# Redo branch ahead of the last mix, gate scores on VectorE, and a newly planned order in a gated scan with top-k experts

## The chip, the cores and the metric

The kernel runs on one core of a Trainium2 chip. Its engines take their instructions from queues of their own, each in the order in which the program wrote them: TensorE (PE, with PEld for its weight loads), VectorE (DVE), ScalarE (ACT), GpSimd (POOL) and SyncE (SP). GpSimd and SyncE issue the transfers here. The metric is device time in microseconds of one execution, as the median of several runs. The kernel before took 221.41 us (three runs, 220.95 to 222.44).

## The reference

```
f = lower_bound + (1 - lower_bound) * sigmoid(f_logit)      # batch 4, seq 6208, 256 channels
h[t] = f[t] * h[t-1] + (1 - f[t]) * x[t]                    # a scan over the sequence, per channel
scores = h @ w_gate                                         # one score for each row, per batch
top = the 128 rows of the batch with the highest scores
ye = relu(h[top] @ w1) @ w2                                 # w1: 256 x 1024, w2: 1024 x 256
out = h;  out[top] = h[top] + sigmoid(scores[top]) * ye
```

All is in float32. The chosen rows are known only when the whole batch has been scanned and scored.

## The kernel before, in words

**Units.** Each batch is cut into units of one to four blocks of 256 rows (`UNITS`, line 27), 29 units in all, numbered 0 to 28; the last units of the batches are 7, 14, 21 and 28. A unit has channels on the partitions, in two halves (`h`). For each unit SP loads `ft` (the logits) and `xt` (x), line 260. ACT makes the sigmoid (L263) and the forget gate `gt` (L267). The input is weighed by `1 - f`: GpSimd does so in two steps (`prepare` L271, `weigh` L275); a share of the first half's columns, given by `SHARE`, is done by VectorE in one step instead (L282); units 0 and 28 are done by VectorE alone (L280). VectorE scans (L285). TensorE makes the scores of each block with a matrix that has the gate weights in one of 32 columns, so that the block lands in a partition of its own (L294). TensorE turns the scanned unit back into rows (`turn`, L301), four 128 x 128 tiles to a PSUM tile; ACT copies them out (`put`, L318), but for units in `EASED` one of these copies is done by VectorE. SP stores the unit (L321; the odd rows at a batch's start, L324).

**Search.** `choose(b)` finds a batch's 128 rows once its last scores are in: `keep` copies the scores (ACT, L383), `lanes` spreads them over 32 lanes (TensorE, L388), VectorE takes the best 14 of each lane (L398 to L413), `row` and `own` bring them to all partitions (L416, L420), VectorE ranks them (L429) and marks the ranks (L435), `pull` collects the row numbers (TensorE, L440), and `finish` writes them as `idx` (L445). `bad` (L447), `tell` (L450) and `flag` (L454, L455) find whether the ranking lacked a row; then `aim` points the results past the output and `tally` counts the batch.

**Experts.** `experts(b)` has GpSimd gather the rows `xe` from the output in memory with an indirect DMA (`fetch`, L483), once the batch's last store has landed. TensorE turns them (L489), ACT copies them (`xT`, L493), TensorE multiplies with `w1` (`up`, L508) and, after the second group, with the gate weights (`ask`, L497, into the same PSUM tile as the turned rows); ACT makes the sigmoid of that (`open`, L501) and the relu (L514); TensorE multiplies with `w2` (`down`, L519). VectorE mixes (`mix`, L523), and GpSimd scatters the result with an indirect DMA (L527). The PSUM tile `acc` is one bank; all searches use it, and so do the `down` products of batches 0, 1 and 3. Batch 2 (`APART`) has a tile of its own for them. A search therefore begins only when the mixes of earlier batches other than 2 are done.

**Redo.** `redo_all` comes after everything: VectorE sums the tally (L605), four engines load the sum (L606) and branch on it (L607). Only if a batch lacked a row is the long body run, which selects the rows one at a time; otherwise it is jumped over. In these runs it is jumped over.

**Order.** The order is planned before the program is written. `Plan.run` places each operation, with its cost, in a simulated time; among the operations that are ready on an engine it takes the one with the lowest rank, and the instructions are then written in the order of the planned starts. A unit `i` has rank `20 i`, its second half 10 more; its transposes and copies have `TURN` and `PUT` more, its store `STORE` more. The search of batch `b` has the rank `20 * last unit + FIND[b]`, its experts `20 * last unit + EXPERT[b]`. `LAND` is the planned time for a gather to land after its issue. Buffers are counted too: 18 large SBUF slots, two PSUM tiles for transposes (`pt`), two for forget gates (`gt`).

Of the kernel before, what the change touches and what calls it, by code (L numbers as in the profile page):

```python
# [27 lines left out]
SHARE = [1, 0.125, 0.625, 1, 1, 0.25, 0.625, 0, 0.5, 0.625, 0.125, 0.125, 0, 0.75, 0, 1, 0, 0.5, 0.375, 0.25, 0.125, 0.75, 0.375, 0, 0.625, 0.625, 0.5, 0.75, 0.375]  # L28
EASED = [0, 1, 2, 4, 5, 7, 8, 12, 13, 15, 16, 18, 20, 21, 22, 24, 25, 26]
# [10 lines left out]
LAND = 4.0  # L40
# [10 lines left out]
TP = 4  # L51
# [4 lines left out]
class Plan:  # L56
# [5 lines left out]
    def add(self, engine, cost, emit, rank, after, key=None, late=0.0, takes=None):  # L62
# [10 lines left out]
    def run(self):  # L73
# [21 lines left out]
        def can(i):  # L95
            t = self.ops[i][6]
            if t is None or t in self.where:
                return ready[i]
            cls, kind = self.kind[t]
            if not spare[cls] or kind in taken and not taken[kind]:  # L100
                return None
            return max(ready[i], min(spare[cls])[0], min(taken[kind]) if kind in taken else 0.0)
# [4 lines left out]
        for done in range(n):  # L107
# [23 lines left out]
            cost, late, tile_ = self.ops[i][1], self.ops[i][5], self.ops[i][6]  # L131
            if tile_ is not None and tile_ not in self.where:
                cls, kind = self.kind[tile_]
                slot = min(spare[cls])
                spare[cls].remove(slot)
                self.where[tile_] = slot[1]
                if kind in taken:
                    taken[kind].remove(min(taken[kind]))
# [31 lines left out]
def gated_scan_moe(tc, xin, fin, lb, wg, w1, w2, outs, cap):  # L170
    nc = tc.nc
    v, a, pe, g = nc.vector, nc.scalar, nc.tensor, nc.gpsimd
    with ExitStack() as ctx:
# [26 lines left out]
        onesf = const.tile([LANE, P], F32, name="onesf")  # L200
# [13 lines left out]
        for t in rows:  # L214
            g.memset(t, 0.0)
        tally = const.tile([P, B], F32, name="tally")
# [401 lines left out]
        for b in range(B):  # L618
            choose(b)
            experts(b)  # L620
# [37 lines left out]
```

## Time and profile before

| | |
|---|---|
| median of three runs | 221.41 us |
| profiled execution, its own time | 223.16 us |
| profiled execution, span from first to last instruction | 221.4 us |
| mean granted TensorE clock | 0.87 |
| busy: PE, DVE, ACT, POOL | 163.2, 164.7, 152.3, 144.9 us |
| moved | 79.68 MB, mean 360 GB/s |

The profile names an engine, the line of the kernel, and output and inputs (`out<-in`) by tile names. A group's line ends in busy time, mean duration of one in ns, and idle time of the engine ahead of it with what ended it. A timeline's line begins with start and length in us; so does the chain of waits, which goes back from the last instruction through whatever released each step. An fp32 product shows as two records for each 128 rows of the contraction. `PEq`, `POOLq` and so on are the engines' sequencers.

### The profile page before, as it was taken

Reading aid. Unit: us, or ns where it says so; the run is one execution under the profiler, and the core shown is the slowest. Engines: PE = TensorE matmul, PEld = TensorE weight load, DVE = VectorE, ACT = ScalarE, POOL = GpSimd, SP = SyncE. Lnnn points to the kernel's source line nnn. Section 1 sums busy time; section 2 is a strip of 40 time slices with the busy share of each in tenths; the row PEclk is TensorE's granted clock in tenths of the full one; section 3 lists DMA queues with packets and bytes.
Section 4 is the critical chain, followed back from the end, with each engine's and each line's share of the span. In section 5 each row is a group of like instructions: output and inputs, shape, how many; then the busy total and the mean of one; then the engine's idle time right before and its main releaser. Section 6 shows DMA issues by size and latency. Waiting matters only on the chain.

```text
span 221.4 us, 3263 instructions
## 1 busy us (share of the span) xinstructions
PE 163.2 (74%) x1132; PEld 108.5 (49%) x1132; DVE 164.7 (74%) x215; ACT 152.3 (69%) x202; POOL 144.9 (65%) x129
## 2 busy tenths in 40 slices
PE   0585787566969296668775799985968999699970
PEld 0232453332535144324543688653638856489850
DVE  1659999576899997699998686799979898740000
ACT  4589987969999569698999747987795425312210
POOL 4479682899999999099999993999991011001110
PEclk9999979988796759997999659995596999958997
DMA  5999999999999999999999999999999985910001
GB/s 160 421 426 426 426 428 419 429 426 420 426 425 417 430 416 426 428 423 429 423 425 420 428 423 428 423 422 419 430 417 426 420 364 213 377 52 24 28 0 31
DMA packets 13828, 79.68 MB, mean 360 GB/s; under 512 B 1904, under 2 KB 2160, under 8 KB 5872
## 3 DMA queue, kind: packets, MB, share of 16 engines
q1 hardware_dynamic: 13136, 78.39, 85.1%
q0 software_dynamic: 384, 1.05, 1.4%
q8 instruction: 10, 0.16, 0.3%
q14 instruction: 10, 0.08, 0.1%
q10 hardware_dynamic: 288, 0.00, 0.1%
HBM read 53.48 MB, written 25.95 MB: 359 GB/s over the span
## 4 chain that ended last, share of the span: by engine, by line
DMA 49%; PE 20%; DVE 12%; POOL 7%; issue 5%; ACT 4%; SPq 0%; POOLq 0%; ACTq 0%; DVEq 0%
DMA xt<-x 24%; PE pm L508 11%; DMA ft<-fl 7%; DMA out<-ym 7%; DMA out<-yt 6%; DVE xt L285 5%; POOL xt L275 4%; PE acc L519 3%; DMA xe<-out,idx 3%; DVE junk L429 3%; DMA wgo<-wg 2%; PE pt L301 2%; PE score L294 2%; PE py L519 2%; POOL xt L271 1%
## 5 line engine op out<-in xcount | busy, mean ns | idle before, releaser
L285 DVE TENSOR_TENSOR_SCAN xt<-gt,xt 128x1024 f32<-128x1024 f32 (+4 forms) x58 | 113.5, 1982 | 13.1 <-POOL xt L275 7.8
L275 POOL TENSOR_TENSOR xt<-xt,ft 128x1024 f32<-128x1024 f32 (+10 forms) x52 | 89.6, 1727 | 5.9 <-ACT ft L263 2.6
L301 PE MATMUL pt<-ident,xt 128*128 128x128 f32 x384 | 73.9, 332 | 11.8 <-ACT ym L318 10.3
L301 PEld LDWEIGHTS pt<-ident,xt 128*128 128x128 f32 x384 | 55.7, 202 | 42.9 <-ACT ym L318 24.9
L294 PE MATMUL score<-xt,wgr 128*32 128x256 f32 (+1 forms) x400 | 44.2, 450 | 30.3 <-DVE xt L285 29.5
L267 ACT ACTIVATE gt<-ft,nl 128x1024 f32<-128x1024 f32 (+4 forms) x58 | 56.8, 985 | 9.5 <-DVE xt L285 9.2
L318 ACT COPY ym<-pt 128x512 f32<-128x512 f32 (+1 forms) x90 | 47.8, 557 | 16.2 <-PE pt L301 15.0
L271 POOL TENSOR_SCALAR xt<-xt,nl 128x1024 f32<-128x1024 f32 (+10 forms) x52 | 45.1, 870 | 19.8 <-DMA xt<-x 7.9
L263 ACT ACTIVATE ft<-ft 128x2048 f32<-128x2048 f32 (+4 forms) x29 | 47.2, 1635 | 7.0 <-DMA ft<-fl 6.9
L294 PEld LDWEIGHTS score<-xt,wgr 128*32 128x32 f32 x400 | 10.0, 116 | 42.4 <-DVE xt L285 29.6
L508 PE MATMUL pm<-xT,w1t 128*128 128x128 f32 x128 | 24.0, 360 | 2.8 <-ACT ym L318 1.8
L508 PEld LDWEIGHTS pm<-xT,w1t 128*128 128x128 f32 x128 | 22.0, 265 | 4.7 <-ACT ym L318 2.4
L282 DVE SCALAR_TENSOR_TENSOR xt<-gt,xt 128x640 f32<-128x640 f32 (+9 forms) x22 | 14.4, 655 | 10.8 <-ACT gt L267 10.7
L483 POOL DMA_INDIRECT xe<-out,idx x4 | 4.4, 1096 | 23.5 <-DVE bad L447 23.2
L527 POOL DMA_INDIRECT out<-res,aim x4 | 4.2, 1053 | 21.3 <-DVE res L523 13.6
L514 ACT ACTIVATE hT<-pm 128x512 f32<-128x512 f32 x8 | 4.8, 597 | 11.8 <-PE pm L508 11.8
L429 DVE TENSOR_SCALAR_CACHE_REDUCE junk<-acc,mine 128x448 bf16<-128x448 f32 x16 | 10.9, 684 | 0.6
L519 PE MATMUL acc<-w2t,hT 128*128 128x256 f32 x48 | 10.9, 379 | 0.0
L519 PEld LDWEIGHTS acc<-w2t,hT 128*128 128x128 f32 x48 | 8.9, 190 | 1.1
L318 DVE COPY ym<-pt 128x512 f32<-128x512 f32 (+1 forms) x14 | 8.6, 615 | 0.0
L523 DVE SCALAR_TENSOR_TENSOR res<-acc,open,xe 128x256 f32<-128x256 f32 x3 | 1.5, 485 | 8.8 <-PE acc L519 8.8
L493 ACT COPY xT<-pm 128x256 f32<-128x256 f32 x4 | 1.5, 378 | 6.3 <-PE pm L489 6.3
(62 smaller groups left out, 65.5 us busy)
## 6 DMA issues: line engine op xcount, KB each, us to landing
ft<-fl SPq DMA_DIRECT2D x20, 1024.0 KB, 16.2
xt<-x SPq DMA_DIRECT2D x20, 1024.0 KB, 15.8
out<-ym SPq DMA_DIRECT2D x20, 1024.0 KB, 14.8
ft<-fl SPq DMA_DIRECT2D x3, 832.0 KB, 15.3
xt<-x SPq DMA_DIRECT2D x3, 832.0 KB, 15.2
out<-ym SPq DMA_DIRECT2D x3, 768.0 KB, 15.5
out<-ym SPq DMA_DIRECT2D x5, 256.0 KB, 17.4
w1t<-w SPq DMA_DIRECT2D x1, 1024.0 KB, 19.6
```

The source lines that it names most:

```text
L263: a.activation(fs[i], fs[i], ACTF.Sigmoid, scale=-1.0)
L267: a.activation(gs[i, h][:, :n], fs[i][:, h], ACTF.Identity, scale=nl[:, h : h + 1], bias=1.0)
L271: g.tensor_scalar(xs[i][:, h, c0:], xs[i][:, h, c0:], nl[:, h : h + 1], 1.0, ALU.mult, ALU.mult)
L275: g.tensor_tensor(xs[i][:, h, c0:], xs[i][:, h, c0:], fs[i][:, h, c0:], ALU.mult)
L282: v.scalar_tensor_tensor(xs[i][:, h, :c1], gs[i, h][:, :c1], 1.0, xs[i][:, h, :c1], ALU.subtract, ALU.mult)
L285: v.tensor_tensor_scan(xs[i][:, h], gs[i, h][:, :n], xs[i][:, h], carry[h] if blk0 else 0.0, ALU.mult, ALU.subtract)
L294: pe.matmul(score[j * CG : (j + 1) * CG, b % 2, c0:], wgr[:, h, r], xs[i][:, h, c + c0 : c + BLK], start=(h == 0 and blk0 + q < 3), stop=( ...
L301: pe.transpose(pts[key][:, q * P : (q + 1) * P], xs[i][:, h, tail + c :: cols], ident)
L318: (v.tensor_copy if eng == "dve" else a.copy)(out, src)
L429: v.tensor_scalar(junk, acc[:, :ROW], st["mine"][:, k : k + 1], None, ALU.is_gt, ALU.add, accum_out=acc[:, A_RANK + k : A_RANK + k + 1])
L508: pe.matmul(st["pm", f // TP][:, c : c + P], w1t[:, h, f * P : (f + 1) * P], st["xT"][:, h], start=(h == 0), stop=(h == NH - 1))
L519: pe.matmul(st["py"][:, :D], st["hT"][:, f], w2t[:, f], start=(f == 0), stop=(f == NF - 1))
```

## The change

Five things are changed at once.

1. **Redo.** `redo_all` becomes an operation of the plan, after batch 3's `down` products and its `ask`; batch 3's `mix` comes after it. The body gets buffers of its own: one large SBUF slot (`spot`) that holds its working tiles, rows, `xT`, `hT` and result, and the two `gt` tiles (`bank`) in place of `pt` and `acc`.
2. **Gate score of the gathered rows.** `ask` becomes a VectorE product of the rows `xe` with a tile `wgrow`, which has the gate weights in a row on every partition, with the sum over the row; its product goes to `res`, which the mix overwrites. TensorE's four products for each batch are gone, and the `w1` products no longer wait for the gate. `wgrow` is made once, near unit 2: VectorE scales an identity by the gate weights (two instructions, into a row buffer), TensorE multiplies it with ones into `acc`, ACT copies it. `lanes` waits for it. `res`, `open` and `gate` have two buffers.
3. **Sliding gate columns.** The seven 32-column score matrices become one of 63 columns with the weights in the middle; a block takes the 32 columns that put the weights in its place.
4. **Planner.** An operation may take several tiles; `ups` take their PSUM tile at the first product of a group; the turned rows' PSUM tile is freed after `xT`, no longer after `open`.
5. **New values** for `SHARE`, `EASED`, `STORE`, `TURN`, `PUT`, `FIND`, `EXPERT`, `WEIGHTS_AT` and `LAND`.

```
-SHARE = [1, 0.125, 0.625, 1, 1, 0.25, 0.625, 0, 0.5, 0.625, 0.125, 0.125, 0, 0.75, 0, 1, 0, 0.5, 0.375, 0.25, 0.125, 0.75, 0.375, 0, 0.625, 0.625, 0.5, 0.75, 0.375]
-EASED = [0, 1, 2, 4, 5, 7, 8, 12, 13, 15, 16, 18, 20, 21, 22, 24, 25, 26]
+SHARE = [0, 1, 0.75, 0.625, 0.75, 0, 0.125, 0.375, 0.75, 0.25, 0, 0, 0.625, 0.625, 0, 0.25, 0.625, 0.25, 0.125, 0.75, 0, 0, 0.375, 0.125, 0, 0.5, 0.25, 0.375, 0]
+EASED = [0, 2, 4, 5, 6, 7, 8, 11, 12, 13, 15, 16, 17, 19, 20, 21, 23, 25, 26, 28]
...
-AHEAD, BACKLOG, STORE = 30.0, 4.0, 200.0
-TURN, PUT, FIND, EXPERT = 25.0, 20.0, [60.0, 100.0, 0.0, -100.0], [240.0, 80.0, 120.0, -100.0]
-WEIGHTS_AT = [4, 4]
+AHEAD, BACKLOG, STORE = 30.0, 4.0, 180.0
+TURN, PUT, FIND, EXPERT = 45.0, 45.0, [80.0, 140.0, -100.0, 40.0], [200.0, 0.0, 240.0, 40.0]
+WEIGHTS_AT = [5, 2]
...
-LAND = 4.0
+LAND = 5.0
...
-        wgr = const.tile([P, NH, NROW, CG], F32, name="wgr")
+        wgr = const.tile([P, NH, 2 * CG - 1], F32, name="wgr")
         g.memset(wgr, 0.0)
-        for r in range(NROW):
-            v.tensor_copy(wgr[:, :, r, r], wgo)
+        v.tensor_copy(wgr[:, :, CG - 1], wgo)
...
-pe.matmul(score[j * CG : (j + 1) * CG, b % 2, c0:], wgr[:, h, r], xs[i][:, h, c + c0 : c + BLK],
+pe.matmul(score[j * CG : (j + 1) * CG, b % 2, c0:], wgr[:, h, CG - 1 - r : 2 * CG - 1 - r], xs[i][:, h, c + c0 : c + BLK],
...
             def fetch():
-                st["xe"] = rows[b % 2]
+                again = "found" in st
+                spot = st.get("spot")
+                st["xe"] = spot[:, 3 * BLK : 4 * BLK] if again else rows[b % 2]
+                st["res"] = spot[:, BLK : 2 * BLK] if again else moe.tile([P, D], F32, name="res", bufs=2)
...
             def ask():
-                for h in range(NH):
-                    pe.matmul(st["px"][:, D : D + 1], st["xT"][:, h], wgo[:, h : h + 1], start=(h == 0), stop=(h == NH - 1))
+                st["gate"] = moe.tile([P, 1], F32, name="gate" + "2" * ("found" in st), bufs=2)
+                v.scalar_tensor_tensor(st["res"], st["xe"], 1.0, wgrow, ALU.mult, ALU.mult, accum_out=st["gate"])
...
-            plan.tile(("pm", b, 0), ("pt", "pt"), [k("open")])
+            plan.tile(("pm", b, 0), ("pt", "pt"), [("xT", b)])
             add("act", 0.38, take, p0 - 1, [k("flip"), prev], ("xT", b))
+            add("dve", 0.6, ask, p0, [k("xe"), prev, ("wgrow",)], k("ask"))
+            add("act", 0.22, opened, p0 - 1, [k("ask")], k("open"))
...
-            add("dve", 0.5, mix, p0 - 1, [k("down", NF - 1), ("scatter", b - 1), k("open")], ("mix", b))
+            add("dve", 0.5, mix, p0 - 1, [("redo",) if b == B - 1 else k("down", NF - 1), ("scatter", b - 1), k("open")], ("mix", b))
...
         def redo(b):
-            number, work, key = [sel.tile([P, BLK], F32, name=n) for n in ("number", "work", "key")]
+            spot = hold(("spot",), [P, 8 * BLK], "spot")
+            bank = [hold(("bank", k), [P, 4 * BLK], "bank") for k in range(2)]
+            number, work, key = [spot[:, k * BLK : (k + 1) * BLK] for k in range(3)]
...
+        def spread_gate():
+            for h in range(NH):
+                v.tensor_scalar(rows[0][:, h * P : (h + 1) * P], ident, wgo[:, h : h + 1], None, ALU.mult)
+
+        def gate_row():
+            pe.matmul(acc[:, :D], onesf, rows[0], start=True, stop=True)
+
+        def keep_row():
+            a.copy(wgrow, acc[:, :D])
...
+        add("pe", 0.0, redo_all, 20.0 * N, [("moe", B - 1, "down", NF - 1), ("moe", B - 1, "ask")], ("redo",), takes=[("spot",), ("bank", 0), ("bank", 1)])
+        add("dve", 0.4, spread_gate, 60.0, [("gate", 2)], ("search", "gate", 0))
+        add("pe", 0.8, gate_row, 60.0, [("search", "gate", 0)], ("search", "gate", 1))
+        add("act", 0.4, keep_row, 60.0, [("search", "gate", 1)], ("wgrow",))
...
         with tc.manual_schedule():
             plan.run()
-            redo_all()
```

More of the change, by code (lines that the diff above doesn't have):

```diff
@@ L60, in __init__, with add @@
         self.kind, self.freed, self.where = {}, {}, {}
-    def add(self, engine, cost, emit, rank, after, key=None, late=0.0, takes=None):
+    def add(self, engine, cost, emit, rank, after, key=None, late=0.0, takes=()):
         if key is not None:
@@ L95, in can @@
         def can(i):
[L96 to L102, printed above, removed]
+            when = ready[i]
+            for t in self.ops[i][6]:
+                if t not in self.where:
+                    cls, kind = self.kind[t]
+                    if not spare[cls] or kind in taken and not taken[kind]:
+                        return None
+                    when = max(when, min(spare[cls])[0], min(taken[kind]) if kind in taken else 0.0)
+            return when
         for i in range(n):
@@ L130, in run @@
             queue[e].remove(i)
[L131 to L138, printed above, removed]
+            cost, late = self.ops[i][1], self.ops[i][5]
+            for x in self.ops[i][6]:
+                if x not in self.where:
+                    cls, kind = self.kind[x]
+                    slot = min(spare[cls])
+                    spare[cls].remove(slot)
+                    self.where[x] = slot[1]
+                    if kind in taken:
+                        taken[kind].remove(min(taken[kind]))
             if e == "pe":
@@ L333, in unit @@
                 q = p + 10 * h
-                add("act", 0.2 + 0.91 * k, lambda h=h: forget(h), q + 1, [("gate", i), ("forget", i - (1 - h), 1 - h)], ("forget", i, h), takes=("gt", i, h))
+                add("act", 0.2 + 0.91 * k, lambda h=h: forget(h), q + 1, [("gate", i), ("forget", i - (1 - h), 1 - h)], ("forget", i, h), takes=[("gt", i, h)])
                 plan.tile(("gt", i, h), ("gt", "gt"), [("scan", i, h)])
@@ L457, in choose @@
             chain("act", 0.4, keep, ("keep", b), extra=[("scores", last_unit[b], 1)])
-            chain("pe", 0.8, lanes, extra=[("flag", b - 1), *[("mix", c) for c in range(b) if c not in APART]])
+            chain("pe", 0.8, lanes, extra=[("flag", b - 1), ("wgrow",), *[("mix", c) for c in range(b) if c not in APART]])
             for k in range(4):
@@ L486, in turn_in @@
             def turn_in():
-                st["px"] = psum(0)
+                st["px"] = st["bank"][1] if "found" in st else hold(("pm", b, 0), [P, TP * P], "pm")
                 for h in range(NH):
@@ L511, in relu @@
             def relu(f0):
-                if f0 == 0:
+                if f0 == 0 and "found" in st:
+                    st["hT"] = st["spot"][:, NF * P : 2 * NF * P].rearrange("p (f e) -> p f e", f=NF)
+                elif f0 == 0:
                     st["hT"] = moe.tile([P, NF, P], F32, name="hT")
@@ L517, in down @@
                 if f == 0:
-                    st["py"] = hold(("py", b), [P, 4 * BLK], "py") if b in APART and "found" not in st else acc
+                    st["py"] = st["bank"][1] if "found" in st else hold(("py", b), [P, 4 * BLK], "py") if b in APART else acc
                 pe.matmul(st["py"][:, :D], st["hT"][:, f], w2t[:, f], start=(f == 0), stop=(f == NF - 1))
             def mix():
-                st["res"] = moe.tile([P, D], F32, name="res")
                 v.scalar_tensor_tensor(st["res"], st["py"][:, :D], st["open"], st["xe"], ALU.mult, ALU.add)
@@ L617, in gated_scan_moe @@
             add("sp", XFER, lambda t=t, src=src, n=n: weights(t, src, n), 20.0 * WEIGHTS_AT[k], [("x", WEIGHTS_AT[k])], ("w", k), late=DONE)
+        plan.tile(("spot",), ("big", "s"), [("redo",)])
+        for k in range(2):
+            plan.tile(("bank", k), ("gt", "gt"), [("redo",)])
+        add("pe", 0.0, redo_all, 20.0 * N, [("moe", B - 1, "down", NF - 1), ("moe", B - 1, "ask")], ("redo",), takes=[("spot",), ("bank", 0), ("bank", 1)])
+        add("dve", 0.4, spread_gate, 60.0, [("gate", 2)], ("search", "gate", 0))
+        add("pe", 0.8, gate_row, 60.0, [("search", "gate", 0)], ("search", "gate", 1))
+        add("act", 0.4, keep_row, 60.0, [("search", "gate", 1)], ("wgrow",))
         for b in range(B):
```

44 lines of the change are left out of this document (22 added, 22 removed).

## The prediction

> **What bounds the kernel now.** First the page, which shows where the limits change. The figures of the second and third line are the 40 slices of 5.5 us.
>
> ```profile
> span 221.4 us, 3263 instructions
> PEclk9999979988796759997999659995596999958997
> DMA  5999999999999999999999999999999985910001
> L275 POOL TENSOR_TENSOR xt<-xt,ft 128x1024 f32<-128x1024 f32 (+10 forms) x52 | 89.6, 1727 | 5.9 <-ACT ft L263 2.6
> L271 POOL TENSOR_SCALAR xt<-xt,nl 128x1024 f32<-128x1024 f32 (+10 forms) x52 | 45.1, 870 | 19.8 <-DMA xt<-x 7.9
> L282 DVE SCALAR_TENSOR_TENSOR xt<-gt,xt 128x640 f32<-128x640 f32 (+9 forms) x22 | 14.4, 655 | 10.8 <-ACT gt L267 10.7
> ```
>
> The transfers fill slices 2 to 32, up to about 177 us; then comes a tail of some 44 us with little traffic. An order that only reshuffles the full stretch cannot gain there; the tail can. So I read the chain that ended last (start, length, what):
>
> ```profile
> 187.35 6.14 DMA xe<-out,idx
> ...
> 193.62 0.42 PE pm L489 x2
> ...
> 196.55 0.65 PE pm L497 x4
> ...
> 201.59 0.08 PE acc L440 x4
> ...
> 205.79 0.23 PE pm L489 x2
> ...
> 207.68 0.34 PE pm L497 x4
> ...
> 214.37 0.48 DVE res L523
> ```
>
> From 193.62 the chain is TensorE: batch 2's experts from 193.62 to 205.79 (12.2 us), batch 3's from 205.79 to 214.28, where the chain hands over to the last mix (8.5 us). The same program takes 3.7 us longer for batch 2. The windows say why; their columns are busy time of PE, PEld, DVE, ACT and POOL, granted clock, DMA share and GB/s:
>
> ```profile
> 187.73:191.15 3.42, 3.19 (x31) 2.47 (x30) 2.45 (x10) 2.52 (x6) 0.65 (x1) 1.00 0.89 346
> 191.15:194.56 3.41, 1.30 (x13) 0.42 (x11) 2.53 (x8) 0.46 (x2) 0.00 (x0) 1.00 0.93 376
> 194.56:197.97 3.41, 3.41 (x16) 3.41 (x17) 1.51 (x5) 0.17 (x1) 0.00 (x0) 0.50 0.03 12
> 197.97:201.38 3.41, 3.41 (x18) 3.41 (x17) 0.00 (x0) 0.60 (x1) 0.00 (x0) 0.50 0.00 0
> 201.38:214.28 12.90, 12.37 (x81) 10.79 (x79) 0.94 (x5) 2.33 (x5) 2.02 (x2) 1.00 0.07 22
> ```
>
> After 191.15 TensorE is nearly out of work: batch 2's gather is late. The two stretches that follow run at half clock, which costs about half of 6.8 us. The DMA share, 0.93 and then 0.03, also shows that the last stores have landed at about 195 to 196. How the gather came to be late stands in the timeline:
>
> ```profile
> 106.12 4.59 DVE L285 TENSOR_TENSOR_SCAN xt<-gt,xt 128x1024 f32<-128x1024 f32 x2
> ...
> 116.67 2.35 DVE L285 TENSOR_TENSOR_SCAN xt<-gt,xt 128x1024 f32<-128x1024 f32 x1
> ...
> 137.38 0.49 DVE L523 SCALAR_TENSOR_TENSOR res<-acc,open,xe 128x256 f32<-128x256 f32 x1
> ...
> 142.00 0.33 DVE L398 MAX8 ci<-acc 32x8 f32<-32x194 f32 x1
> ...
> 176.04 0.48 DVE L523 SCALAR_TENSOR_TENSOR res<-acc,open,xe 128x256 f32<-128x256 f32 x1 [0.82 <-PE acc L519]
> ...
> 178.47 0.35 DVE L398 MAX8 ci<-acc 32x8 f32<-32x194 f32 x1
> ...
> 181.09 0.73 DVE L285 TENSOR_TENSOR_SCAN xt<-gt,xt 128x256 f32<-128x256 f32 x1
> ...
> 182.33 0.14 DVE L425 COPY mine<-acc 128x4 f32<-128x4 f32 x1
> ...
> 186.92 0.15 DVE L445 TENSOR_REDUCE idx<-acc 128x1 int32<-128x2 f32 x1
> ...
> 195.46 0.68 DVE L435 TENSOR_TENSOR hot<-slot,acc 128x512 bf16<-128x512 bf16 x1
> ...
> 201.71 0.16 DVE L445 TENSOR_REDUCE idx<-acc 128x1 int32<-128x2 f32 x1 [5.57 <-PE acc L440]
> ```
>
> One PSUM bank carries the searches and the results of batches 0, 1 and 3, so they go in a row: mix 0 (137.38), search 1 (from 142.00), mix 1 (176.04), search 2 (178.47 to 187.1), gather 2. Search 3 has its marks ready at 196.14 (195.46 + 0.68), but its pull stands in TensorE's order behind batch 2's up products and runs at 201.59: 5.4 us lost.
>
> **The change part by part.**
>
> *New ranks.* EXPERT[0] falls by 40, two units of 20. The scans at 106.12 (unit 17) and 116.67 (unit 19) price two units at 10.55 us. Gather 0 now follows unit 19's rank:
>
> ```profile
> 113.18 1.23 POOL L483 DMA_INDIRECT xe<-out,idx  x1 [0.18 <-issue]
> ...
> 189.84 0.99 PE L301 MATMUL pt<-ident,xt 128*128 128x128 f32 x4 [0.23 <-ACT ym L318]
> ...
> 202.14 1.00 POOL L483 DMA_INDIRECT xe<-out,idx  x1 [13.76 <-DVE bad L447]
> ...
> 206.66 1.02 POOL L527 DMA_INDIRECT out<-res,aim  x1 [3.51 <-DVE res L523]
> ```
>
> So I move gather 0, and mix 0, some 10.5 us forward, to about 127. FIND[1] rises by 40, to unit 21's rank, so search 1 begins near 130, not 142. EXPERT[1] falls by 80, and FIND[2] by 100: both already outranked everything near them, and I give them nothing. From search 1 to mix 1 took 34 us; kept, mix 1 comes at about 164, and search 2's index at about 175 (it took 10.9 from mix to index). Gather 2 leaves 8 to 12 us earlier. It needs only about 3 to be there when TensorE ends the last transposes (189.84 + 0.99 = 190.8). TensorE then runs batch 2 without the gap: 8.5 us at full clock, less 0.34 for the gate product, and 0.5 that I allow for search 3's own small products (the pull is 0.08 in the chain): 199.5.
>
> Gather 3: marks at 196.14, a hop of 0.1, 0.55 from pull to issue (201.59 to 202.14), so issue by 196.8, and that is after the last stores. Behind up products the pull can lose 0 to 5.4 us; LAND now plans a gather 6.4 us long (1.04 + 0.36 + 5), near the 6.1 of gather 2, where it planned 5.4, so I take 1.0, the time of half a group of up products. Landings, from issue:
>
> ```profile
> xe<-out,idx POOLq DMA_INDIRECT x1, 7.7
> ...
> xe<-out,idx POOLq DMA_INDIRECT x1, 2.8
> ...
> out<-res,aim POOLq DMA_INDIRECT x1, 3.1
> ...
> out<-res,aim POOLq DMA_INDIRECT x1, 4.2
> ```
>
> These are gather 0, gather 3, scatter 2 and scatter 3. With 2.8, and 0.13 from landing to the first product (187.35 + 6.14 to 193.62), batch 3's products start at 196.8 + 1.0 + 2.8 + 0.1 = 200.7, against 205.79 now: **5.1 us gained**. The bounds of the pull make it 6.1 and 0.7.
>
> *Gate on VectorE.* The four gate products leave TensorE (0.65 and 0.34 in the chain); batch 3's 0.34 counts beside the sum above. VectorE gains four products of two 128x256 operands, each near the mix's 0.48; in the tail it has that time. The new product waits for its gather at the head of VectorE's queue: 7.7 against a planned 6.4 is up to 1.3 us, with scans and search steps queued behind it, and TensorE's score products and ACT's next gates waiting for those. The L282 row has VectorE idle for 10.8 us ahead of its own steps, which absorbs it; uncovered, two times 1.3 for the two gathers under full transfers. The one-time row of gate weights is four small instructions near unit 2, under full transfers; the first search, which now waits for it, comes much later: nothing; uncovered 1 to 1.5 us.
>
> *Branch before the last mix.* Its rows now:
>
> ```profile
> L607 POOLq COMPARE_BRANCH  x1: 53/53/53, 215.5 to 215.5; - x1
> L607 POOLq EVENT_SEMAPHORE  x5: 17/43/43, 218.3 to 219.3; - x5
> ...
> L654 SPq EVENT_SEMAPHORE  x14: 17/28/28, 219.7 to 221.3; - x14
> ```
>
> GpSimd needs 2.7 us from branch to its next instruction, and its last wait at 219.3 is for scatter 3 (4.2 after its issue). Behind the branch stand only the last mix on VectorE and the last scatter on GpSimd; SP has no part in it. Early in the queue, all this lies beside batch 3's products: the tally is ready near 203, and GpSimd is free from 207.7 (206.66 + 1.02) and done by about 211.5, the mix being no earlier than 214 now. Batches 2 and 3 move together, so the cover of about 3 us stays; without it the jump adds up to 2.7. What goes: the semaphore step between landing and the final waits (219.3 to 219.7, 0.4 to 0.5), and the instruction fetch under scatter 3, whose landing took 4.2 beside scatter 2's 3.1: 1.1. **1.6 us gained**, bounds 0.4 to 1.6. [...]
>
> *SHARE.* Outside the two direct units it sums to 10,784 columns on VectorE before, 8,576 after. At 14.4 us for 10,784, VectorE loses 2.9 us of work. GpSimd has 134.7 us for 37,700 columns (all 49,664, less the shared ones and 1,152 of the direct units), so it gains 7.9, of which 5.0 for units 24 to 27 (1,408 columns); there it works out of the chain after 167. EASED adds two copies to VectorE and takes them from ACT. Zero, cover as named. *Sliding columns*: six copies fewer at the start, under the loads: zero. *STORE, TURN, PUT, WEIGHTS_AT*: zero while transfers are full; the bound is in the third rival.
>
> Sum: 5.1 + 0.34 + 1.6 = 7.0; span 214.4. The profiled execution took 223.16 in all, 1.75 above the median of 221.41; the same difference from the median gives **214.4**.
>
> **The rivals.** *The order buys nothing.* Gathers and the pull stay as late. For it: nine lists and constants change at once, and priorities bind only among ready work. Then only direct terms remain, 1.6 + 0.34 + 0.65 = 2.6: 218.8.
>
> *TensorE cools.* Batch 2 ends before gather 3 lands and TensorE waits. The windows show that 1.30 us of work in 3.41 halves the next two. Batch 3's products then cost about 3.4 more: 217.8. [...]
>
> *Paid ahead of the last scan: slower.* The rest of search 2 (182.33 to 187.1, about 4.9 us) is pulled before the last scan at 181.09, and TURN and PUT, 20 and 25 later, leave one more unit's copies and its 1 MB store behind (3.0 us at the 346 GB/s of the first window). The last store lands near 195.5 + 4.9 + 3.0 = 203.4, batch 3's products start at about 206.4; cold (8.15 + 3.4) they bring the last mix to 218.0, and its own 7.0 (214.37 to 221.4) less 1.6 remain: 223.4, or 1 to 2 more where VectorE also stands for gathers. I put it at 224.4. It decides once the last store lands after about 202. Against it: VectorE's idle 10.8 us, and the 2.9 that SHARE takes off it.
>
> **How the numbers follow.** Forecast 0.40 (own range 211 to 217); order buys nothing 0.26; cold TensorE 0.13; paid ahead 0.16; 0.05 for better still, search 3 also earlier, down to 209. Measurement tells 1% (2.2 us) from no change: below 219.2 and above 223.6. Forecast, cold, better and half of the second rival are faster: 0.40 + 0.13 + 0.05 + 0.13, less 0.07 for late parts of each: 0.64. Slower: most of the third, 0.14. Same: 0.22. The range 210 to 224 leaves out 0.05 below and about 0.12 above.
>
> **What would show it.** Right: batch 2's gather issued before 184; no half clock between 191 and 201; pull 3 within 1.5 us of its marks; GpSimd's branch before the last mix; scatter 3 landing in about 3.1 and the end within 2 us of it. Wrong: gather 2 still after 187, the last store landing after 202, or GpSimd's scatter starting over 0.5 us after the mix.

## The result, and the profile after

The changed kernel takes 213.9 us (median of four runs, 213.7 to 214.15) against 221.18 us for the kernel before, run beside it (220.2 to 222.44). The ratio is 0.9668, with a 95% interval of 0.9617 to 0.972. The change gains about 7.3 us. The forecast was 214.4.

The page of the changed kernel, with the rows that answer to those shown of the kernel before (in the second and third line a digit stands for 5.3 us). The lines of the kernel are shifted by two to seven.

```profile
span 211.8 us, 3227 instructions
PEclk9998555999966996599699999957996999997998
DMA  6999999999999999999999999999999999892010
L277 POOL TENSOR_TENSOR xt<-xt,ft 128x1024 f32<-128x1024 f32 (+9 forms) x53 | 94.7, 1787 | 4.4
L284 DVE SCALAR_TENSOR_TENSOR xt<-gt,xt 128x640 f32<-128x640 f32 (+9 forms) x20 | 11.8, 588 | 3.4 <-ACT gt L269 3.3
```

The traffic is the same 79.68 MB. Now it is full to slice 34 (180 us) and close to it, 8 and 9, to slice 36 (191 us). Before, it was full to slice 32 (177 us), and then came 8, 5 and 9 up to 194 us: the hole ahead of the last stores is gone. The tail without traffic behind them is 21 us in place of 28. VectorE's share of the weighing fell from 14.4 to 11.8 us, and GpSimd's second step of it rose from 89.6 to 94.7.

This is the same kernel's timeline (start, length, engine, line, operation; in brackets the idle time before it and what ended it), with the events of the gathers, searches and batches that the reading below uses:

```profile
101.73 1.23 POOL L485 DMA_INDIRECT xe<-out,idx  x1 [0.18 <-issue]
...
124.61 0.46 DVE L530 SCALAR_TENSOR_TENSOR res<-acc,open,xe 128x256 f32<-128x256 f32 x1
...
133.69 0.33 DVE L400 MAX8 ci<-acc 32x8 f32<-32x194 f32 x1
...
170.72 0.47 DVE L530 SCALAR_TENSOR_TENSOR res<-acc,open,xe 128x256 f32<-128x256 f32 x1
...
181.60 0.74 DVE L287 TENSOR_TENSOR_SCAN xt<-gt,xt 128x256 f32<-128x256 f32 x1
...
182.67 1.04 POOL L485 DMA_INDIRECT xe<-out,idx  x1 [10.09 <-DMA out<-ym]
...
183.05 0.37 ACT L385 COPY wide<-score 128x256 f32<-128x256 f32 x1
...
183.24 0.15 DVE L457 COPY tally<-acc 128x1 f32<-128x1 f32 x1
...
184.06 0.69 PE L390 MATMUL acc<-order,wide 128*32 128x24 f32 x16
...
189.15 0.41 PE L491 MATMUL pm<-ident,xe 128*128 128x128 f32 x2 [0.53 <-ACT ym L320]
...
191.68 0.68 DVE L437 TENSOR_TENSOR hot<-slot,acc 128x512 bf16<-128x512 bf16 x1
...
192.75 0.29 PE L442 MATMUL acc<-vals,hot 128*128 128x3 bf16 x4
...
193.07 0.16 DVE L447 TENSOR_REDUCE idx<-acc 128x1 int32<-128x2 f32 x1 [0.38 <-PE acc L442]
...
195.44 1.01 POOL L485 DMA_INDIRECT xe<-out,idx  x1 [11.74 <-DMA out<-ym]
...
198.89 0.38 PE L491 MATMUL pm<-ident,xe 128*128 128x128 f32 x2
...
207.20 0.48 DVE L530 SCALAR_TENSOR_TENSOR res<-acc,open,xe 128x256 f32<-128x256 f32 x1 [7.15 <-PEq L615]
207.96 1.00 POOL L534 DMA_INDIRECT out<-res,aim  x1 [7.01 <-DVE res L530]
```

Read down it against the kernel before: gather 0 came 11.5 us earlier (101.73, before 113.18), mix 0 12.8 (124.61, before 137.38), search 1 8.3 (133.69, before 142.00), mix 1 5.3 (170.72, before 176.04), gather 2 4.7 (182.67, before 187.35). The last scan did not move (181.60, before 181.09). But the marks of search 3 are ready at 192.36 (191.68 + 0.68) and not at 196.14, and its `pull` runs 0.4 us behind them and not 5.4. Batch 3's rows come on TensorE at 198.89, where they came at 205.63 (the prediction's chain has that step at 205.79). Batch 2's rows waited for ACT's last copy of scanned rows, which ends at 189.04, and for their gather, which lands at about 189.0 (182.67 and 6.3 from issue to landing): the two came together. Gather 3 had its list at 193.2 and waited until 195.4 for the last stores.

The windows, cut at the steps of the clock (busy time of PE, PEld, DVE, ACT and POOL, granted clock, DMA share, GB/s):

```profile
186.32:189.73 3.41, 2.72 (x20) 1.50 (x19) 2.51 (x8) 1.54 (x5) 0.00 (x0) 1.00 1.01 414
189.73:193.14 3.41, 3.12 (x17) 3.06 (x18) 2.93 (x11) 0.45 (x2) 0.00 (x0) 0.50 0.58 235
193.14:207.20 14.06, 13.43 (x87) 11.95 (x87) 1.27 (x8) 2.97 (x6) 2.03 (x2) 1.00 0.08 24
```

One stretch of 3.4 us at half clock is left in batch 2's products; before there were two. Last, the branch and the end of the program, by line (durations in ns, then first and last start):

```profile
L615 POOLq COMPARE_BRANCH  x1: 53/53/53, 200.7 to 200.7; - x1
...
L615 POOLq EVENT_SEMAPHORE  x5: 17/43/43, 203.5 to 203.8; - x5
...
L678 SPq EVENT_SEMAPHORE  x14: 17/28/28, 204.2 to 211.7; - x14
```

and the last scatter from issue to landing, from the transfers between 207 and 212:

```profile
out<-res,aim POOLq DMA_INDIRECT x1, 2.4
```

GpSimd still takes 2.8 us from the branch to its next instruction, now beside batch 3's products: it is through at about 204.3, 3 us ahead of the mix. The mix starts 0.12 after the last `down` product (ends at about 207.1), as before. From the mix to the end of the span it is 4.6 us (207.20 to 211.8), before 7.0.

Between the two profiled executions 9.6 us of span are gone: batch 3's rows 6.7 earlier, batch 3's own products 0.4 shorter (8.31 from rows to mix, before 8.74), the tail 2.4 shorter. The first profiled execution lay 1.75 above its median, the second at its median; between medians it is 7.3.

### The profile page after: what moved, and what is told of

The parts are those of the page before. It is cut to its first block, busy times and chain, and to the rows that moved or that the text cites. A ratio compares the mean times of both kernels' runs of the same rounds, so it can differ in the third digit from the quotient of the medians.

```text
span 211.8 us, 3227 instructions
## 1 busy us (share of the span) xinstructions
PE 156.1 (74%) x1118; PEld 101.0 (48%) x1118; DVE 167.8 (79%) x219; ACT 151.8 (72%) x201; POOL 152.6 (72%) x131
## 2 busy tenths in 40 slices
DMA packets 13828, 79.68 MB, mean 376 GB/s; under 512 B 1905, under 2 KB 2161, under 8 KB 5873
## 5 line engine op out<-in xcount | busy, mean ns | idle before, releaser
L287 DVE TENSOR_TENSOR_SCAN xt<-gt,xt 128x1024 f32<-128x1024 f32 (+4 forms) x58 | 114.6, 1986 | 14.8 <-POOL xt L277 10.4
L277 POOL TENSOR_TENSOR xt<-xt,ft 128x1024 f32<-128x1024 f32 (+9 forms) x53 | 94.7, 1787 | 4.4
L296 PE MATMUL score<-xt,wgr 128*32 128x256 f32 (+1 forms) x400 | 43.3, 446 | 28.1 <-DVE xt L287 23.5
L273 POOL TENSOR_SCALAR xt<-xt,nl 128x1024 f32<-128x1024 f32 (+9 forms) x53 | 47.9, 903 | 17.3 <-DMA xt<-x 11.1
L320 ACT COPY ym<-pt 128x512 f32<-128x512 f32 (+1 forms) x88 | 46.4, 550 | 14.5 <-PE pt L303 13.6
L265 ACT ACTIVATE ft<-ft 128x2048 f32<-128x2048 f32 (+4 forms) x29 | 47.3, 1630 | 11.8 <-DMA ft<-fl 10.7
L514 PE MATMUL pm<-xT,w1t 128*128 128x128 f32 x128 | 18.2, 303 | 1.7 <-ACT xT L498 1.5
L514 PEld LDWEIGHTS pm<-xT,w1t 128*128 128x128 f32 x128 | 17.0, 214 | 3.0 <-ACT xT L498 2.2
L284 DVE SCALAR_TENSOR_TENSOR xt<-gt,xt 128x640 f32<-128x640 f32 (+9 forms) x20 | 11.8, 588 | 3.4 <-ACT gt L269 3.3
L320 DVE COPY ym<-pt 128x512 f32<-128x512 f32 (+1 forms) x16 | 10.2, 637 | 0.3 <-PE pt L303 0.3
L418 PE MATMUL acc<-dg,onesf 32*128 32x448 f32 x8 | 4.1, 586 | 1.1 <-DVE dg L410 1.1
```

Of the source, the lines that this page charges most:

```text
L265: a.activation(fs[i], fs[i], ACTF.Sigmoid, scale=-1.0)
L273: g.tensor_scalar(xs[i][:, h, c0:], xs[i][:, h, c0:], nl[:, h : h + 1], 1.0, ALU.mult, ALU.mult)
L277: g.tensor_tensor(xs[i][:, h, c0:], xs[i][:, h, c0:], fs[i][:, h, c0:], ALU.mult)
L284: v.scalar_tensor_tensor(xs[i][:, h, :c1], gs[i, h][:, :c1], 1.0, xs[i][:, h, :c1], ALU.subtract, ALU.mult)
L287: v.tensor_tensor_scan(xs[i][:, h], gs[i, h][:, :n], xs[i][:, h], carry[h] if blk0 else 0.0, ALU.mult, ALU.subtract)
L296: pe.matmul(score[j * CG : (j + 1) * CG, b % 2, c0:], wgr[:, h, CG - 1 - r : 2 * CG - 1 - r], xs[i][:, h, c + c0 : c + BLK], start=(h == 0 ...
```

## The experiments

Twelve runs, in three groups, each beside runs of the kernel before (medians 221.35, 221.27 and 221.63). Ratios are to those. Four causes stand against each other: the branch alone, the new order (the ranks, or the shares of work in them), the full clock in batch 2's products, and a difference that only the profiled execution of before had.

### Parts alone

**The branch alone**: the kernel before, with `redo_all` ahead of the last mix and buffers of its own; gate, matrices, constants and written order up to the tail as before.

```
...
+        add("pe", 0.0, redo_all, 20.0 * N, [("moe", B - 1, "down", NF - 1), ("moe", B - 1, "ask")], ("redo",), takes=[("spot",), ("bank", 0), ("bank", 1)])
...
-            redo_all()
```

> The kernel before in its own order, with nothing but the redo branch (and the buffers it needs) moved ahead of the last mix. Theory A (the prediction): the branch, its instruction fetch and its semaphore step leave the end; from the last mix to the end 7.0 us become 4.6 to 5.4, so 1.6 to 2.4 us faster, about 219. Rival B (the end is only the scatter's landing, the branch lay beside it): no change, 221.2. Rival C (the branch makes the last mix wait): up to 2.7 us slower.

Measured: 217.63 us, ratio 0.9831 (0.9741 to 0.992). Its last mix and scatter in its timeline:

```profile
209.84 0.48 DVE L530 SCALAR_TENSOR_TENSOR res<-acc,open,xe 128x256 f32<-128x256 f32 x1 [7.94 <-PEq L616]
210.61 1.00 POOL L534 DMA_INDIRECT out<-res,aim  x1 [7.46 <-DVE res L530]
```

and the scatter from issue to landing, in its transfers from 210 on:

```profile
out<-res,aim POOLq DMA_INDIRECT x1, 2.4
```

From mix to end it is 4.62 (span 214.5), and the scatter lands in 2.4. The gain of 3.7 by the medians is more than the tail's 2.4, but the interval of the ratio, 1.8 to 5.7 us, holds both. In this execution batch 2 also met less of the half clock: from its rows to batch 3's it takes 10.4 us (190.73 to 201.10), where the first profile of the kernel before has 12.0. Its four `ask` records take 0.85 us, as at half clock there, but the twenty `up` records behind them 3.29, before 4.53. Its order up to the tail is that of before, so the rest is not shown to be the branch's.

**The gate alone**: the kernel before with `ask` on VectorE and `wgrow`.

```
...
-                for h in range(NH):
-                    pe.matmul(st["px"][:, D : D + 1], st["xT"][:, h], wgo[:, h : h + 1], start=(h == 0), stop=(h == NH - 1))
...
+                v.scalar_tensor_tensor(st["res"], st["xe"], 1.0, wgrow, ALU.mult, ALU.mult, accum_out=st["gate"])
...
```

> The kernel before with nothing but the gate score of the gathered rows on VectorE (with its row of weights); old ranks, so the planner's order shifts a little. Theory A: four products fewer in each batch's chain, 0.3 us of batch 3's and up to 0.65 of batch 2's: 0.3 to 1.0 us faster, 220.2 to 220.9. Rival (VectorE stands at the head of its queue for a gather): slower by 1 us or more, with a wait of a VectorE gate product on a gather in the trace.

Measured: 221.32 us, ratio 1.0011 (0.997 to 1.0053): nothing. The timeline of batch 3 shows why the 0.34 us that TensorE saves didn't come through:

```profile
202.03 0.38 PE L491 MATMUL pm<-ident,xe 128*128 128x128 f32 x2
...
203.17 0.20 ACT L503 ACTIVATE open<-gate 128x1 f32<-128x1 f32 x1 [3.80 <-DVE res L499]
203.28 0.35 ACT L495 COPY xT<-pm 128x256 f32<-128x256 f32 x1
...
203.69 2.50 PE L510 MATMUL pm<-xT,w1t 128*128 128x128 f32 x20 [1.27 <-ACT xT L495]
```

In ACT's queue the gate's sigmoid (`open`) now stands ahead of the copy `xT`, and waits for VectorE, which is busy with the mix of batch 2. TensorE has its turned rows at 202.4 and its `xT` at 203.6. Batch 3 takes 9.07 from rows to mix, 0.3 more than before. In the changed kernel's timeline the copy comes first:

```profile
199.36 0.37 ACT L498 COPY xT<-pm 128x256 f32<-128x256 f32 x1 [3.13 <-PE pm L491]
...
200.03 0.20 ACT L506 ACTIVATE open<-gate 128x1 f32<-128x1 f32 x1 [0.29 <-DVE res L502]
```

There it takes 8.31. The gate's sign hangs on that one place in ACT's order, and all fourteen traces agree: batch 3 takes 9.06 or 9.07 where `open` stands first (gate alone, and three kernels below: new code with the old constants, old shares, `LAND` at 4), 8.31 where the copy does (changed, branch last, fillers, old ranks), and 8.74 on the old code.

**All the code, none of the new constants**, and **all the constants on the old code**: `SHARE` to `LAND` exchanged between the two kernels.

```
-TURN, PUT, FIND, EXPERT = 45.0, 45.0, [80.0, 140.0, -100.0, 40.0], [200.0, 0.0, 240.0, 40.0]
+TURN, PUT, FIND, EXPERT = 25.0, 20.0, [60.0, 100.0, 0.0, -100.0], [240.0, 80.0, 120.0, -100.0]
```

(and the lines of `SHARE`, `EASED`, `STORE`, `WEIGHTS_AT` and `LAND` in the same way; the other kernel has the reverse.)

> The kernel after, with all the constants of the order as before (SHARE, EASED, STORE, TURN, PUT, FIND, EXPERT, WEIGHTS_AT, LAND). Theory A (the order carries most of the gain): only the direct terms remain, 2.0 to 3.4 us faster than before, 217.8 to 219.2, and batch 2's gather is issued near 187 again. Rival D (the new structure carries it, the order is free): about 214.

> The kernel before with the new constants of the order and nothing else. Theory A: 4 to 5 us faster, 216 to 217, with batch 2's gather issued before 184. Rival D: 221.

Measured: the code with the old constants 217.71 us, ratio 0.9841 (0.9766 to 0.9916); the old code with the new constants 220.89, ratio 0.998 (0.9939 to 1.002). On the new code the constants are worth 3.8 us (217.71 to 213.9), on the old code nothing that can be told. Of the 3.8, 0.75 is the place of `xT` in ACT's order (9.06 against 8.31 from rows to mix). The constants paid only with the operations they were planned with: on the old code the same ranks have search 3's marks ready at 196.05 and batch 3's rows at 202.54, on the new code at 192.36 and 198.89. Nor is a full clock enough: in that trace of the old code batch 2's products run without the half clock (the four `ask` records in 0.50 us, the last sixteen `up` records in 2.03; in the kernel before, at half clock, it is 0.85 for the four and 4.53 for twenty `up` records), and yet its median can't be told apart from that of the kernel before.

### The clock, the pull, and the profiled execution

**The kernel before once more**, unchanged, and **the pull earlier**: the kernel before with three of batch 2's `up` products (and so those behind them) written behind search 3's `pull`.

```
+        for f in (4, 5, 6):
+            start[self.at["moe", 2, "up", f]] = start[self.at["pull", 3]] + 1e-6 * f
```

> The kernel before, unchanged, profiled once more: its own spread. If the half clock in batch 2's products is a matter of where the clock's stretches of 3.41 us happen to fall, batch 2's products (first transposed rows to batch 3's) take about 10 us here, not 12.2, with one half-clock stretch in them, not two, and the time is near the median of 221.3, not the 223.2 of the first profile. If the late gather always costs two stretches, 12 us again.

> The kernel before, with three of batch 2's eight up products moved behind batch 3's pull, so that the pull waits for four and not for seven of them; nothing else. Gather 3 is issued 1 to 3 us earlier. Theory E (TensorE's own work from batch 2's rows to batch 3's decides, the pull only matters once that is shorter): no change, 221 (within 0.5 us). Theory of the prediction's sum, in which the pull is what holds batch 3's products back: 1 to 3 us faster.

Measured: before again 222.38 us (one run). The idea that the two half-clock stretches were an accident of the first profile alone fell; they are there again, in these windows, and batch 2 takes 12.0 us again:

```profile
190.58:193.99 3.41, 1.30 (x13) 0.46 (x12) 2.49 (x8) 0.42 (x2) 0.00 (x0) 1.00 0.94 380
193.99:197.40 3.41, 3.41 (x17) 3.41 (x18) 1.51 (x4) 0.17 (x1) 0.00 (x0) 0.50 0.02 10
197.40:200.82 3.42, 3.42 (x18) 3.36 (x18) 0.00 (x0) 0.60 (x1) 0.00 (x0) 0.50 0.00 0
```

Batch 2 doesn't take that long in every execution: in the branch-alone kernel, with the same order, it is 10.4 us.

With the pull earlier: 221.45 us, ratio 0.9991 (0.9946 to 1.0037). Its pull, gather 3 and batch 3's rows in its timeline:

```profile
197.30 0.29 PE L442 MATMUL acc<-vals,hot 128*128 128x3 bf16 x4
...
198.06 1.00 POOL L485 DMA_INDIRECT xe<-out,idx  x1 [11.29 <-DVE bad L449]
...
203.90 0.38 PE L491 MATMUL pm<-ident,xe 128*128 128x128 f32 x2
```

Gather 3 goes out 6.1 us behind batch 2's rows (192.00), where it was 8.5 in the first profile, so 2.5 us are won there. Batch 3's rows come 5.84 us behind the gather, since TensorE still has batch 2's remaining products to do, the first of them slowed by the half clock (sixteen `up` records from 197.45 on take 3.04 us, against 2.03 in the old code with the new constants). So the 5.4 us for which the pull stood in the queue were not a loss by themselves: of those products the program needs every one, ahead of the pull or behind it.

**Fillers**: three products of 128x512 without use ahead of batch 2's rows in the kernel before, two in the changed kernel. They keep TensorE busy while the gather is under way; their result is overwritten.

```
+                if "found" not in st and b in (2,):
+                    for _ in range(3):
+                        pe.matmul(st["px"], ident, w1t[:, 0, : TP * P], start=True, stop=True)
```

> The kernel before, with three filler products of 128x512 on TensorE ahead of batch 2's transposed rows, where it stands idle for the late gather; the order is the same otherwise. The clock price by itself: if the late gather's half clock costs, then the stretch after the gather keeps the full clock and batch 2's products take 8.5 to 9 us: 1 to 3.4 us faster, 218 to 220. If the clock is not what makes batch 2 long, or the filler delays the rows as much as it saves, no change.

> The kernel after, with two filler products on TensorE ahead of batch 2's transposed rows. One half-clock stretch is left there (189.7 to 193.1), worth 1.7 us on TensorE. Theory E (after the change, TensorE, the last stores and search 3 end within 1 us of each other: gather 3 is issued only after the last store, at 195.4, lands at 198.2, and TensorE is free for it at 198.9): at most 0.7 us faster, and no change or slower by the filler's own length where the rows are there already. Rival (TensorE's clock alone sets the tail still): 1.7 us faster, 212.2.

Measured: in the kernel before 219.22 us, ratio 0.9923 (0.9891 to 0.9955). TensorE's timeline in that kernel:

```profile
193.31 2.84 PE L490 MATMUL pm<-w1t,ident 128*128 128x512 f32 x6
195.99 0.38 PE L492 MATMUL pm<-ident,xe 128*128 128x128 f32 x2
```

and its windows:

```profile
193.77:197.18 3.41, 2.95 (x11) 1.40 (x10) 3.27 (x10) 0.37 (x1) 0.00 (x0) 1.00 0.58 233
197.18:200.60 3.42, 3.42 (x36) 3.41 (x35) 0.36 (x1) 0.77 (x2) 0.00 (x0) 1.00 0.00 0
```

The clock stays at 1.00, and batch 2 takes 8.7 us (195.99 to 204.70) where it took 12.0: **3.3 us is the price of the two half-clock stretches**. The fillers cost part of it: the gather lands at about 193.8 (188.75 and 5.1), and batch 2's rows come only at 195.99. In the changed kernel they change nothing: 213.71 us, ratio 0.9671 (0.9584 to 0.9758), though batch 2 now runs at full clock (1.00 from 189.40 to 199.00) in 8.27 us and not 9.74. That alone doesn't show that its one stretch at half clock was covered, for the fillers also hold the rows up by 1.0 us (the gather lands at about 189.7, the rows come at 190.86). The next table shows that it was, and by what.

### What sets the start of batch 3

From the traces, in us (start of the first record): batch 2's rows on TensorE, search 3's marks ready, its `pull`, gather 3's issue, batch 3's rows.

| kernel | batch 2's rows | marks 3 | pull 3 (`up` products of batch 2 ahead of it, of 32 records) | gather 3 | batch 3's rows |
|---|---|---|---|---|---|
| before | 193.62 | 196.14 | 201.43 (28) | 202.14 | 205.63 |
| before with fillers | 195.99 | 197.55 | 200.50 (28) | 201.22 | 204.70 |
| new code, old constants | 192.23 | 196.47 | 196.75 (16) | 197.46 | 202.28 |
| new code, old ranks | 191.99 | 194.93 | 195.04 (12) | 197.94 | 201.88 |
| new code, old shares | 192.33 | 196.22 | 198.08 (28) | 198.80 | 202.28 |
| changed | 189.15 | 192.36 | 192.75 (12) | 195.44 | 198.89 |
| changed, branch last | 189.74 | 193.63 | 193.68 (12) | 195.54 | 199.68 |
| changed, fillers | 190.86 | 193.04 | 193.15 (12) | 195.91 | 199.13 |

In the last three rows, which have one order on TensorE, batch 3's rows come 6.14, 6.00 and 5.98 us behind the pull: the rest of batch 2's products, at full clock but for 0.4 us in the changed kernel. The pull itself follows the marks within 0.4. So there the marks of search 3 set the end, and half clock ahead of the pull costs nothing as long as the products ahead of it end with the marks. The changed kernel with the branch last shows the other face of it: it has no half clock there (1.00 from 186.50 to 199.70), and TensorE waits instead, as its timeline shows:

```profile
193.68 0.25 PE L442 MATMUL acc<-vals,hot 128*128 128x3 bf16 x4 [1.44 <-DVE hot L437]
```

In the kernel before TensorE was the later one, by 5.3 us (201.43 against 196.14).

### The parts of the order

**Old ranks**: the changed kernel with the old `FIND` and `EXPERT` alone; all other constants stay new. **Old shares**: the changed kernel with the old `SHARE` and `EASED` alone.

```
-TURN, PUT, FIND, EXPERT = 45.0, 45.0, [80.0, 140.0, -100.0, 40.0], [200.0, 0.0, 240.0, 40.0]
+TURN, PUT, FIND, EXPERT = 45.0, 45.0, [60.0, 100.0, 0.0, -100.0], [240.0, 80.0, 120.0, -100.0]
```

> The kernel after with only TURN and PUT new and FIND and EXPERT as before. If the new ranks of searches and experts are what brings batch 2's gather forward (182.7 in the kernel after, 185.0 with all old constants), the gather is at 185 or later again and the time 216 to 218. If it is SHARE, EASED and STORE, it stays near 214.

> The kernel after, with SHARE and EASED as before. The ranks of searches and experts carry 2.5 of the 3.8 us that the new order is worth on the new structure (216.4 and 217.7 against 213.9). If the split between VectorE and GpSimd carries the rest, about 1.3 us slower, 215.2, with batch 2's gather still near 183; if it carries nothing, 214; if ranks and shares only work together, as late as with the old ranks, 216 to 218.

Measured: old ranks 216.41 us, ratio 0.9771 (0.9708 to 0.9835); old shares 215.88, ratio 0.976 (0.9674 to 0.9847). By the medians the ranks are worth 2.5 us and the shares 2.0; both intervals touch that of the changed kernel. The two don't add up to the 3.8 of all constants, and the traces show a reason. Search 3 begins on TensorE with `lanes`, which waits for two things: the end of search 2's flag (the copy to `tally`), since both searches use the one bank, and the end of `keep`, ACT's copy of the last scores. In us:

| kernel | `tally` of search 2 ends | `keep` of search 3 ends | `lanes` of search 3 starts | marks 3 |
|---|---|---|---|---|
| before | 187.62 | 186.58 | 187.84 | 196.14 |
| changed | 183.39 | 183.42 | 184.06 | 192.36 |
| new code, old ranks | 186.21 | 183.42 | 186.39 | 194.93 |
| new code, old shares | 183.26 | 187.30 | 187.92 | 196.22 |
| new code, old constants | 185.66 | 186.87 | 187.28 | 196.47 |

The rows of the kernel before in its timeline:

```profile
186.21 0.37 ACT L383 COPY wide<-score 128x256 f32<-128x256 f32 x1 [0.84 <-PE score L294]
...
187.47 0.15 DVE L455 COPY tally<-acc 128x1 f32<-128x1 f32 x1
...
187.84 0.69 PE L388 MATMUL acc<-order,wide 128*32 128x24 f32 x16
```

those of the one with the old ranks:

```profile
186.06 0.15 DVE L457 COPY tally<-acc 128x1 f32<-128x1 f32 x1
...
186.39 0.69 PE L390 MATMUL acc<-order,wide 128*32 128x24 f32 x16
```

and those of the one with the old shares, from the last scan on:

```profile
184.35 0.75 DVE L287 TENSOR_TENSOR_SCAN xt<-gt,xt 128x256 f32<-128x256 f32 x1
...
186.93 0.37 ACT L385 COPY wide<-score 128x256 f32<-128x256 f32 x1
...
187.92 0.69 PE L390 MATMUL acc<-order,wide 128*32 128x24 f32 x16
```

The old ranks delay search 2 alone (gather 2 leaves at 185.59, against 182.67), the old shares the last scores alone, and the later of the two sets `lanes`. So the losses don't add, and a gain in one is worth only as much as the other allows. With the old shares gather 2 goes out at the same time (182.64), but VectorE comes to the last scan 2.75 us later (184.35, against 181.60) and `keep` starts 3.9 later (186.93, against 183.05). VectorE has no time to spare ahead of that scan, as the windows of this run show (VectorE is the third busy time):

```profile
160.00:170.00 10.00, 10.00 (x71) 8.88 (x71) 9.90 (x9) 8.36 (x10) 8.22 (x7) 0.87 1.02 423
170.00:180.00 10.00, 8.18 (x88) 5.16 (x87) 9.72 (x21) 4.73 (x10) 1.10 (x1) 1.00 0.94 388
```

The traced execution with the old shares, 217.75 us, is the slowest of five and 1.9 above their median, and 0.75 of it is again the place of `xT`; so the sizes in this trace are larger than what the medians give.

**LAND at 4** in place of 5, all else as changed.

```
-LAND = 5.0
+LAND = 4.0
```

> The kernel after, planned with LAND 4 in place of 5. If planning for late gathers is what keeps products and pulls from standing behind a gather, 1 to 3 us slower, with longer waits of TensorE or VectorE for a gather's landing. If LAND is one draw of the planner's order among others, within 1 us.

Measured: 214.2 us, ratio 0.9724 (0.9621 to 0.9827): as the changed kernel. `pull` 3 stands behind all 32 `up` records there, gather 2 leaves at 180.66, batch 3's rows come at 198.50, and batch 3 itself takes 9.06, since `open` again stands ahead of `xT`. Two orders that differ in many places end within 0.3 us.

### The branch, taken back

The changed kernel with its order and buffers, but the branch written after everything.

```
...
-        add("pe", 0.0, redo_all, 20.0 * N, [("moe", B - 1, "down", NF - 1), ("moe", B - 1, "ask")], ("redo",), takes=[("spot",), ("bank", 0), ("bank", 1)])
+        add("pe", 0.0, lambda: None, 20.0 * N, [("moe", B - 1, "down", NF - 1), ("moe", B - 1, "ask")], ("redo",), takes=[("spot",), ("bank", 0), ("bank", 1)])
...
         with tc.manual_schedule():
             plan.run()
+            redo_all()
```

> The kernel after, with the redo branch put back behind the last scatter; the planned order is the same. The mirror of the first run, at the other end. If the branch is a fixed price behind the last mix (7.0 us to the end against 4.6), it costs 2.4 us here too: 216.3. If it was worth more in the first run for another reason (3.7 us in the medians there), 217.5 or more; if the gain needed the old tail, 214.

Measured: 217.42 us, ratio 0.9845 (0.9751 to 0.9939), 3.5 us slower than the changed kernel. Its mix is at 207.99 and the span ends at 215.8: 7.85, against 4.61. The last scatter, in the transfers from 207 on:

```profile
out<-res,aim POOLq DMA_INDIRECT x1, 4.5
```

Over all traces, the stretch from the last mix to the end is 6.58 to 7.85 us with the branch behind it (seven traces, mean 7.09) and 4.61 or 4.62 with the branch ahead (seven). **By the tail the branch is worth 2.5 us**; where the medians say 3.5 to 3.7, the tails of those two pairs of traces bear 2.4 to 3.2. The scatter lands in 4.2 us (before) and 4.5 (branch last) in the one case, and in 2.4 in the other (changed, branch alone).

## Why the prediction was right, and where its steps were not

The time was right: 7.0 forecast, 7.3 measured. The split was not, and that the sum fits is in part luck. Of the 7.3 between medians the traces give some 2.4 to the tail and 0.4 to batch 3's products, which leaves about 4.5 for batch 3's earlier start; the forecast had 1.6, 0.34 and 5.1. The branch was 0.8 too small and the start 0.6 too large, and the two misses offset each other.

- **Gather 0, mix 0, search 1.** Forecast: 10.5 earlier, mix 0 at about 127, search 1 near 130. Measured: 11.5 earlier, 124.61, 133.69. Right in kind; search 1 gained 8.3 of its 12.
- **"From search 1 to mix 1 took 34 us; kept"**: it took 37.0 (133.69 to 170.72). So gather 2 leaves 4.7 us earlier and not 8 to 12. About 3 were needed, as the prediction said. The transposes too ended earlier, at 188.63, and the gather landed at about 189.0, so batch 2's rows came at 189.15 where 190.8 was forecast, and the gather had no time to spare.
- **No half clock between 191 and 201**: wrong. One stretch stayed, 189.73 to 193.14. It cost no time, since the pull still ran 0.4 behind the marks. Batch 2 took 9.7 and not 8.7.
- **Marks at 196.14**: this is the step that failed. The prediction kept search 3's time and looked for the gain in the pull (5.4 lost, 1.0 after). But a pull moved alone gained nothing (221.45 us): the products behind which it had stood still had to be done. What made room was search 3, with marks 3.8 us earlier, together with batch 2 on TensorE 4.5 us earlier. The prediction had the row of the one bank (mix 0, search 1, mix 1, search 2) and ended it with gather 2, but search 3 stands in that row too: its `lanes` came 3.8 earlier (184.06, before 187.84) because search 2's flag came 4.2 earlier and the last scores were copied 3.2 earlier. It gave "search 3 also earlier" 0.05, as a way down to 209; that case came, and the time was 213.9.
- **SHARE and EASED: zero**: wrong. With the old ones the marks come 3.9 us later in the trace and the time is 2.0 longer by the medians. The prediction had counted what VectorE loses (2.9 us of work) and set it against idle time, a sum over the span; with the old shares VectorE is busy for 9.90 of 10 us from 160 to 170 and 9.72 from 170 to 180, and there nothing covers it. The two lists were exchanged together, so which of them carries it is open.
- **Gather 3 after the last stores**: the pull was 0.4 behind the marks, within the 1.5 named, but the gather then waited 2.2 us for the last stores (193.2 to 195.4). It lands at 198.2, when TensorE has its last products of batch 2 to do (until 198.9). Marks with batch 2's rest, and stores with the gather, end within 1 us of each other.
- **The order's term**: 5.1 forecast for batch 3's start, about 4.5 measured by the division above. The new constants alone are worth 3.8 between medians (217.71 to 213.9); in the traces 3.4 of that is batch 3's start (202.28 to 198.89) and 0.75 the place of `xT`. So about 1 us of the earlier start goes with the new code and not with the order; which part of the code it is was not tried.
- **Gate 0.34**: 0.43 in the changed kernel's trace (8.74 to 8.31 from rows to mix), but nothing alone, since the copy `xT` had to be ahead of `open` in ACT's queue. The prediction didn't see this place.
- **Branch 1.6, bounds 0.4 to 1.6**: 2.5, beyond the bound. The step was the 1.1 for the scatter, from 4.2 to scatter 2's 3.1. With nothing beside it a scatter lands in 2.4, so 1.8 to 2.1 are gained there, and the semaphore step (0.5) with it. The nearest row was not a clean one: scatter 2 of the kernel before had two instruction fetches beside it (from 207.5). The cover of about 3 us was there (204.3 to 207.2).
- **The rivals.** "The order buys nothing" would have been 218.8; the new code with the old constants, 217.71, is about that case, and the new constants on the old code show that it was a real one. "TensorE cools" didn't occur in batch 3: its products ran at 1.00 from 193.14 on. "Paid ahead of the last scan" didn't occur: the last scan came only 0.5 later (181.60), and the last store's packets ended at 194.1, 2.0 earlier than before.
- **Zero for the rest.** `LAND` is within 0.3 us. The sliding columns, `STORE`, `TURN`, `PUT` and `WEIGHTS_AT` were not tried alone.

What stays open: why the medians give the branch 3.5 to 3.7 us where the tails give 2.4 to 3.2. In both pairs of traces the remaining time lies upstream of the last mix, in work that the branch doesn't touch, and with the branch alone the interval (1.8 to 5.7 us) is wide enough to hold either value.

## What to carry to other kernels

Before you count a wait in an in-order queue as lost, ask what the engine does meanwhile: if it is work that must be done anyway, moving the waiting instruction gains nothing, and it is the later one of the two chains that has to move. Where a step waits for two inputs, look which comes last, because a gain in the other is worth only as much as that one allows. The planned priorities paid here only with the code they were planned for, so measure both together, and try the constants on the old code and the new code on the old constants before you credit either. Put a taken branch where the engines have other work still to wait for (here GpSimd needed 2.8 us from it to its next instruction), and take the price of a transfer from one that has nothing beside it (here 2.4 us for the scatter, against 3.1 to 4.5 with instruction fetches beside it).

## What the runs showed of the hardware

**Half clock after part of a stretch's work.** A stretch of 3.41 us with 1.30 us of TensorE work was followed by two at 0.50, in both profiled executions of the kernel before; with 2.95 us (the fillers) the clock stayed at 1.00. In the changed kernel a stretch with 2.72 us of work was followed by half clock too (186.32 to 189.73), while one with 1.99 us (152.18 to 155.59) was followed by full clock in the same trace, so busy time alone doesn't settle it. What the chip counts stays open.

**Instruction fetches go with a slow transfer.** From the branch to its next instruction GpSimd needs 2.8 us in the kernel before (215.5 to 218.3) and in the changed kernel (200.7 to 203.5), 2.9 with the branch alone (202.5 to 205.4), and 4.1 in the changed kernel with the branch last (209.4 to 213.5, until just after the scatter's landing). With the branch behind it, the last scatter, of 128 rows, lands in 4.2 us (before) and 4.5 (branch last), and four instruction fetches, packets of the queues that the profile names `instruction`, run beside it in each; with the branch done earlier it lands in 2.4 (changed, branch alone), and none do. Scatter 2 of the changed kernel, with GpSimd's branch right behind it (199.93, then 200.7), took 3.3 us with three fetches beside it. It need not be the branch: scatter 2 of the kernel before took 3.1 us with two fetches beside it and no branch. That the fetches are the cause is argued from this and not proven.
